# A weight tile's low half subtracted on GpSimd, and three bias groups of the second chunk moved into the first stage

## The chip, the cores and the metric

The kernel runs on one core of a Trainium2 chip. The metric is the device time of one execution in microseconds; a kernel's time is the median over its runs. Engines are named as in the profile: PE is TensorE's matmul side and PEld its weight loads, DVE is VectorE, ACT is ScalarE, POOL is GpSimd, SP issues all of this kernel's DMAs.

## What is computed

The reference is attention with a learned position bias, followed by two gated feed-forward layers:

```python
def _attn_ref(q, k, v, w1, b1, w2):            # q, k, v: (4, 8, 576, 64)
    scores = scale * np.matmul(q, k.transpose(0, 1, 3, 2))
    x = (psi_rel / psi_i)[..., None]           # from log1p of the positions alone
    h = np.maximum(x @ w1 + b1, 0.0)           # 32 hidden values for each pair of positions
    bias = h @ w2
    scores = scores + bias.transpose(2, 0, 1)[None, :, :, :]
    attn = np.exp(scores - np.max(scores, axis=-1, keepdims=True))
    attn = attn / (np.sum(attn, axis=-1, keepdims=True) + 1e-09)
    return np.matmul(attn, v)
def _moe_ref(x, w_gate, w_val, w_out):         # d_model 512, d_ff 1536
    return ((1.0 / (1.0 + np.exp(-(x @ w_gate)))) * (x @ w_val)) @ w_out
def _moe2_ref(x, w_in, w_out):                 # d_ff 2048
    h = x @ w_in
    return (h * np.clip(h + 3.0, 0.0, 6.0) / 6.0) @ w_out
```

The weights of the two layers are 64-bit floats in memory; the kernel converts them on the chip.

## The kernel before

The 576 query positions are cut into five chunks (128, 128, 128, 128, 64 positions; `QC`). For a chunk, attention has 16 units, each a pair of heads of one batch entry, and the feed-forward part has 68 steps (`STEPS`). A step multiplies one weight tile of 512 by 128 with the chunk's 512 tokens. Every operand is kept as two 32-bit halves, a high one (`xyh`, `gh`, `wp[:, 0]`) and a low one (`xyl`, `gl`, `wp[:, 1]`), so a step is 4 x 3 = 12 matmuls (`product`, L362).

The program has a **lead** and five blocks. In the lead, which an order written out by hand fixes on PE, ACT, DVE and SP, the bias of chunk 0 is computed in eight groups of 16 positions: `bias_hidden` (two relu tiles on ACT, L123, and two on DVE, L125), `bias_mm` (8 matmuls, L134, which the trace records as 16), `bias_out` (out of PSUM by ACT, L146, for chunk 1, and by DVE, L148, for the others, then a DMA to DRAM). `bias_read` fetches it back as tile `bm`. Then come chunk 0's 16 attention units: `att_qk` (L226), `att_min` (DVE, L241, from PSUM, with `bm`), `att_exp` (ACT, L251), `att_norm` (DVE, L258 to L261), `att_tr` (transposes L274, copies L277), `att_av` (L293) and `att_x` (L309, L310). 

Block k runs the 68 steps of chunk k. Between steps, a list of events (`block_events`) places the attention units of chunk k+1 and its bias; only PE's order is fixed by hand there, and the other engines' order is made by a scheduler. In block 0 each weight tile is also converted. `w_load` fetches the raw tile `wd` (pool `wf`), and `w_split` makes `wp` out of it: a scaled copy on ACT (L335), a shift and two bit operations on DVE (L336, L337, L340) in a work tile `cm`, of which there are two, then the high half on ACT (L345) and the low half on DVE (L346). `wp` (six buffers) is what the step's matmuls read; a DMA also writes it to DRAM (`wsp`, L347), from where the blocks 1 to 4 load it. Step i waits for tile i.

Conversions of tiles 0 and 1 stand in the lead, between the first `att_qk` and the first `att_min`. The tiles from 2 on belong to block 0, but the scheduler already puts some of them beside the lead's last units. PSUM holds two two-bank buffers (`s_ps`) for the bias groups and the scores, and four one-bank buffers for everything else.

Of the kernel before, what the change touches and what calls it, by code (L numbers as in the profile page):

```python
# [9 lines left out]
F32 = mybir.dt.float32  # L10
# [3 lines left out]
ALU = mybir.AluOpType  # L14
# [10 lines left out]
QC = ((0, 128), (128, 128), (256, 128), (384, 128), (512, 64))  # L25
# [30 lines left out]
def fused_kernel(ctx: ExitStack, tc: tile.TileContext, qd, kd, vd, tz, rd, zc, w2b, iden, wpack, out):  # L56
    nc = tc.nc
# [36 lines left out]
    t0 = S - QC[0][1]  # L94
# [65 lines left out]
    def bias_read(u):  # L160
        c, hp, b = u
        n = QC[c][1]
        if b == 0:
            bm = bm_p.tile([128, 2, S], F32, name="bm")
            for p in range(0, NQ, n):
                nc.sync.dma_start(out=bm[p:p + n], in_=biasD[c][:, 2 * hp:2 * hp + 2, :])
            bm_q[c, hp] = bm
# [159 lines left out]
    def w_split(n):  # L327

        if n >= NSTEP:
            return  # L330
        wd = wf_q.pop(n)
        low, high = wd[:, :, 0], wd[:, :, 1]
        m = A["cv"].tile([128, 512], U32, name="cm")
        f = m.bitcast(F32)
        nc.scalar.activation(out=f, in_=high.bitcast(F32), func=AF.Copy, scale=2.0 ** -112)  # L335
        nc.vector.tensor_scalar(out=m, in0=m, scalar1=3, scalar2=None, op0=ALU.logical_shift_left)  # L336
        nc.vector.scalar_tensor_tensor(  # L337
            out=m, in0=low, scalar=29, in1=m, op0=ALU.logical_shift_right, op1=ALU.bitwise_or
        )
        nc.vector.scalar_tensor_tensor(  # L340
            out=m, in0=high, scalar=0x80000000, in1=m, op0=ALU.bitwise_and, op1=ALU.bitwise_or
        )
        wp = w_p.tile([128, 2, 4, 128], F32R, name="wp")
        wv = wp.rearrange("p s c m -> p s (c m)")
        nc.scalar.activation(out=wv[:, 0], in_=f, func=AF.Copy)  # L345
        nc.vector.tensor_tensor(out=wv[:, 1], in0=f, in1=wv[:, 0].bitcast(F32), op=ALU.subtract)  # L346
        nc.sync.dma_start(out=wsp[n], in_=wv.bitcast(F32))  # L347
        wq[n] = wp

# [77 lines left out]
    ET = mybir.EngineType  # L427
    us = units[0]
    NL = len(us)
    with ExitStack() as lead:  # L430
        for name, bufs in (("s", 3), ("k", 6), ("v", 7), ("wf", 2), ("cv", 2)):
            A[name] = lead.enter_context(tc.tile_pool(name=name + "l", bufs=bufs))
        lead.enter_context(tc.manual_schedule(engines={ET.PE, ET.Activation, ET.DVE, ET.SP}))
        nc.sync.dma_start(out=id_t, in_=iden)
        for n in range(2):
            w_load(n)
        for u in us[0:3]:
            att_load(u, False)
        nc.sync.dma_start(out=tz_t[:, 0:t0], in_=tz[:, 0:t0])
        for G in range(QC[0][1] // 16 + 1):  # L440
            if G < QC[0][1] // 16:
                for g in range(4):
                    bias_hidden(G, g)
                bias_mm(G)
            if G:
                bias_out(G - 1)
        bias_read(us[0])
        att_qk(us[0])
        for n in range(2):
            w_split(n)  # L450
        att_min(us[0])
        att_qk(us[1])
        for n in range(NL + 2):
            if n + 3 < NL:
                att_load(us[n + 3])
            if n < NL:
                att_exp(us[n])
            if n + 1 < NL:
                att_min(us[n + 1])
            if 1 <= n <= NL:  # L460
                for part in range(3):
                    att_tr(us[n - 1], part, mm_ps)
            if n < NL:
                att_norm(us[n])
            if n >= 2:
                att_av(us[n - 2], mm_ps)
                att_x(us[n - 2])
            if n + 2 < NL:
                att_qk(us[n + 2])
            if n == NL - 4:  # L470
                gate = issued[0]

# [9 lines left out]
    for n in range(2, WA):  # L482
        w_load(n)

    def chunk_bias(c, t0, dt):

        i0, n = QC[c]
        G0, nG = i0 // 16, n // 16
        ev = []
        for g in range(nG):  # L490
            ev.append((t0 + dt * g, lambda G=G0 + g: [bias_hidden(G, t) for t in range(4)]))
        for g in range(0, nG, 2):
            def outs(G=G0 + g):
                for i in range(2):
                    bias_mm(G + i)
                for i in range(2):
                    bias_out(G + i)
            ev.append((t0 + dt * g + dt + 1, outs))
        return ev
# [24 lines left out]
    def block_events(k):  # L524
        ev = []
        last = NSTEP - 1
        if k < 2:
            ev += chunk_bias(k + 1, 2.0, 1.5)
            t0 = 21.0
            ev += chunk_att(k + 1, t0, last, 2)  # L530
        elif k + 1 < NC:
            ev += chunk_att(k + 1, 0.5, last, len(units[k + 1]) // 8)
        if 0 < k < NC - 2:
            ev += chunk_bias(k + 2, *((22.0, 5.2) if k == 1 else (4.0, 12.0)))
        return [e[::2] for e in sorted((e[0], n, e[1]) for n, e in enumerate(ev))]
# [79 lines left out]
```

## Time and profile before

| | us |
|---|---|
| median of 3 runs | 1197.76 (1196.39 to 1198.26) |
| the profiled execution's own time | 1193.32 |
| its span | 1191.2 |
| PE busy in the span | 1155.7 |
| DVE busy | 637.2 |
| ACT busy | 569.0 |
| POOL busy | 0.2 |

The profiled execution is 2.1 us longer than its span, and 4.4 us faster than the median. Busy time is a sum over stages that have different limits; a matmul's end is modelled, so that a busy PE is not necessarily PE at its peak.

### The profile page before, as it was taken

To read this page: it belongs to the slowest core of one execution; us is meant where nothing else is said; L and a number is where in the kernel's file an instruction comes from. 1 tells how busy PE (TensorE), PEld (TensorE's weight loads), DVE (VectorE), ACT (ScalarE), POOL (GpSimd) and SP (SyncE) were. 2 spreads that over 40 slices of the span, in tenths; PEclk is the share of its full clock that TensorE was granted. 3 is DMA by queue.
4 is the path that set the end of the run, shared out by engine and by line. 5 is a ranking of instruction groups with operands and counts; after the bars stand their busy time and mean duration, and the time that the engine had idled before them with its cause. 6 is when DMAs were issued, how large, how long until landed. Compare 5 with 4: busy or idle time off the path is not lost.

```text
span 1191.2 us, 20173 instructions
## 1 busy us (share of the span) xinstructions
PE 1155.7 (97%) x7676; PEld 926.0 (78%) x7676; DVE 637.2 (53%) x1384; ACT 569.0 (48%) x1153; POOL 0.2 (0%) x4
## 2 busy tenths in 40 slices
PE   5898998999999999999999999999999999999998
PEld 2666776777777787787788878878878878888998
DVE  6787888999973544574634453453323314231232
ACT  6686866677662434565633453443323314331231
POOL 0000000000000000000000000000000000000000
PEclk9899999999999999999999999999999999999999
DMA  6787899998977667676686666566677677658997
GB/s 228 275 308 257 306 328 323 365 342 313 338 263 236 205 227 224 194 226 199 188 272 196 213 194 218 187 215 192 188 230 234 208 239 220 212 167 257 368 365 275
DMA packets 115263, 297.64 MB, mean 250 GB/s; under 512 B 20448, under 2 KB 35168, under 8 KB 115168
## 3 DMA queue, kind: packets, MB, share of 16 engines
q1 hardware_dynamic: 115168, 296.36, 75.4%
q8 instruction: 61, 1.00, 0.3%
q14 instruction: 34, 0.28, 0.1%
HBM read 245.32 MB, written 50.99 MB: 249 GB/s over the span
## 4 chain that ended last, share of the span: by engine, by line
PE 83%; DVE 8%; DMA 5%; ACT 2%; issue 2%; SPq 0%; DVEq 0%; ACTq 0%
PE ps L362 63%; PE ps L293 6%; PE ps L274 5%; DMA wd<-wpack 3%; PE ps L226 3%; PE ps L210 3%; PE ps L134 2%; DVE cm L337 2%; DVE cm L340 1%; DVE wp L346 1%; DVE s L241 1%; ACT cm L335 1%; DMA wsp<-wp 1%; DVE cm L336 1%; DVE s L261 0%
## 5 line engine op out<-in xcount | busy, mean ns | idle before, releaser
L362 PE MATMUL ps<-xyh,wp 128*128 128x512 f32 (+1 forms) x1600 | 480.6, 375 | 0.0
L362 PE MATMUL ps<-gh,wp 128*128 128x512 f32 (+1 forms) x1120 | 345.7, 379 | 0.0
L362 PEld LDWEIGHTS ps<-xyh,wp 128*128 128x128 f32 x1600 | 290.5, 189 | 59.5 <-issue 8.2
L362 PE MATMUL ps<-xyl,wp 128*128 128x512 f32 (+1 forms) x800 | 295.0, 369 | 0.7 <-DVE xyl L375 0.7
L362 PEld LDWEIGHTS ps<-gh,wp 128*128 128x128 f32 x1120 | 204.1, 189 | 40.6 <-issue 6.4
L362 PE MATMUL ps<-gl,wp 128*128 128x512 f32 (+1 forms) x560 | 207.1, 370 | 0.0
L362 PEld LDWEIGHTS ps<-xyl,wp 128*128 128x128 f32 x800 | 151.2, 189 | 23.3 <-DVE xyl L375 1.1
L277 ACT ACTIVATE pT<-ps 128x384 f32<-128x384 f32 x216 | 101.4, 487 | 114.2 <-PE ps L274 113.7
L371 ACT ACTIVATE gh<-tmp 128x512 fp32r<-128x512 f32 (+1 forms) x140 | 82.3, 588 | 110.4 <-DVE tmp L393 76.7
L251 ACT ACTIVATE s<-s,m 128x576 f32<-128x576 f32 x144 | 110.5, 769 | 41.8 <-DVE m L241 41.7
L373 DVE TENSOR_TENSOR gl<-tmp,gh 128x512 fp32r<-128x512 f32 (+1 forms) x140 | 89.2, 637 | 62.7 <-ACT gh L371 62.4
L362 PEld LDWEIGHTS ps<-gl,wp 128*128 128x128 f32 x560 | 106.3, 190 | 14.9
L241 DVE CUSTOM_DVE_ANT_0 s<-ps,bm 128x576 f32<-128x576 f32 x144 | 103.8, 754 | 26.1 <-PE ps L226 13.5
L274 PE MATMUL ps<-id_t,s 128*128 128x128 f32 x648 | 102.6, 277 | 11.6 <-DVE s L261 10.2
L274 PEld LDWEIGHTS ps<-id_t,s 128*128 128x128 f32 x648 | 79.1, 141 | 43.2 <-issue 9.3
L293 PE MATMUL ps<-pT,vt 128*64 128x128 f32 (+1 forms) x1600 | 95.3, 267 | 1.0 <-ACT pT L277 1.0
L393 DVE SCALAR_TENSOR_TENSOR tmp<-tmp,ps 128x512 f32<-128x512 f32 (+1 forms) x60 | 38.0, 633 | 108.3 <-PE ps L362 107.3
L293 PEld LDWEIGHTS ps<-pT,vt 128*64 128x64 f32 x1600 | 78.7, 137 | 20.0 <-issue 14.4
L310 DVE TENSOR_TENSOR xyl<-ps,xyh 128x128 fp32r<-128x128 f32 x72 | 20.8, 289 | 117.0 <-ACT xyh L309 117.0
L399 DVE SCALAR_TENSOR_TENSOR tmp<-tmp,ps 128x512 f32<-128x512 f32 (+1 forms) x80 | 50.6, 632 | 60.8 <-ACT tmp L398 59.2
L261 DVE TENSOR_SCALAR s<-s,r 128x576 f32<-128x576 f32 x144 | 68.3, 516 | 1.9
L389 ACT ACTIVATE tmp<-ps 128x512 f32<-128x512 f32 (+1 forms) x60 | 33.2, 554 | 74.1 <-PE ps L362 72.1
(45 smaller groups left out, 857.0 us busy)
## 6 DMA issues: line engine op xcount, KB each, us to landing
wp<-wsp SPq DMA_DIRECT2D x272, 512.0 KB, 4.3
wd<-wpack SPq DMA_DIRECT2D x68, 512.0 KB, 5.6
wsp<-wp SPq DMA_DIRECT2D x68, 512.0 KB, 5.6
vt<-vd SPq DMA_DIRECT2D x80, 320.0 KB, 4.2
kt<-kd SPq DMA_DIRECT2D x80, 288.0 KB, 4.5
biasD<-bo SPq DMA_DIRECT2D x36, 288.0 KB, 2.7
bm<-biasD SPq DMA_DIRECT2D x16, 576.0 KB, 4.7
qt<-qd SPq DMA_DIRECT2D x16, 256.0 KB, 5.7
```

What stands on the lines that cost most here:

```text
L210: nc.tensor.matmul(out=ps[h][:, j, 0:NI], lhsT=x[r, b, :], rhs=y[r, NI * j:NI * j + NI], start=(i == 0), stop=(i == 2), tile_position=(64 ...
L241: nc.vector.tensor_tensor_reduce(out=d["s"][:, h].rearrange("p (a j) -> p a j", a=2), in0=ps[h][:, :, 0:NI], in1=bm[:, h].rearrange("p (a ...
L251: nc.scalar.activation(out=s[:, h], in_=s[:, h], func=AF.Exp, scale=-1.0, bias=d["m"][:, h:h + 1], accum_out=r[:, h:h + 1],)
L261: nc.vector.tensor_scalar(out=s[:, h], in0=s[:, h], scalar1=r[:, h:h + 1], scalar2=None, op0=ALU.mult)
L274: nc.tensor.transpose(out=ps[:, t * NQ:t * NQ + NQ], in_=p[:, 128 * k:128 * k + 128], identity=id_t)
L277: nc.scalar.activation(out=d["pt"][:, 3 * part:3 * part + 3], in_=ps[:, 0:3 * NQ].rearrange("p (t n) -> p t n", t=3), func=AF.Copy,)
L293: nc.tensor.matmul(out=po[64 * h:64 * h + 64, n * a:n * a + n], lhsT=vt[:, v], rhs=pt[:, k, n * a:n * a + n], start=(t == 0), stop=(t == 4 ...
L362: nc.tensor.matmul(out=ps[:, 0:nt], lhsT=w[:, c, :], rhs=x[:, 0:nt], start=(first and c == 0 and i == 0), stop=(last and c == 3 and i == 2),)
L371: nc.scalar.activation(out=hi[:, 0:nt], in_=src, func=AF.Copy, scale=scale)
L373: nc.vector.tensor_tensor(out=lo[:, 0:nt], in0=src, in1=hi[:, 0:nt].bitcast(F32), op=ALU.subtract)
L393: nc.vector.scalar_tensor_tensor(out=th, in0=th, scalar=1.0, in1=ps, op0=ALU.add, op1=ALU.mult)
L399: nc.vector.scalar_tensor_tensor(out=t, in0=t, scalar=6.0, in1=ps, op0=ALU.min, op1=ALU.mult)
```

## The change

The subtract that makes the low half (L346) goes from DVE to GpSimd, for all 68 tiles. In the lead, the first three of chunk 1's eight bias groups follow chunk 0's eight; block 0 then computes the other five, and its attention events start at step 16 where they started at step 21. The two conversions of the lead move from its beginning to its last two iterations. `NG0` is 8.

```diff
-        nc.vector.tensor_tensor(out=wv[:, 1], in0=f, in1=wv[:, 0].bitcast(F32), op=ALU.subtract)
+        nc.gpsimd.tensor_tensor(out=wv[:, 1], in0=f, in1=wv[:, 0].bitcast(F32), op=ALU.subtract)
...
+    NG0, NG1 = QC[0][1] // 16, 3
...
-        for G in range(QC[0][1] // 16 + 1):
-            if G < QC[0][1] // 16:
+        for G in range(NG0 + NG1 + 1):
+            if G < NG0 + NG1:
                 for g in range(4):
                     bias_hidden(G, g)
                 bias_mm(G)
             if G:
                 bias_out(G - 1)
-        bias_read(us[0])
+            if G == NG0:
+                bias_read(us[0])
         att_qk(us[0])
-        for n in range(2):
-            w_split(n)
         att_min(us[0])
...
                 att_qk(us[n + 2])
+            if n >= NL:
+                w_split(n - NL)
...
-    def chunk_bias(c, t0, dt):
+    def chunk_bias(c, t0, dt, done=0):
...
-        G0, nG = i0 // 16, n // 16
+        G0, nG = i0 // 16 + done, n // 16 - done
...
-            ev += chunk_bias(k + 1, 2.0, 1.5)
-            t0 = 21.0
+            ev += chunk_bias(k + 1, 2.0, 1.5, 0 if k else NG1)
+            t0 = 21.0 if k else 16.0
             ev += chunk_att(k + 1, t0, last, 2)
```

At the beginning of the lead, PE's order (L134 are the bias groups' matmuls, L226 the scores of the first units, L274 the transposes of unit 0), before with - and now with +:

```order
 L105 MATMUL ps<-zc_t,w2b_t 32x2 x2
-L134 MATMUL ps<-z,w2b_t 32x288 x64
+L134 MATMUL ps<-z,w2b_t 32x288 x88
 L226 MATMUL ps<-kt,qt 128x288 x12
 L274 MATMUL ps<-id_t,s 128x128 x9
```

The 24 matmuls of three groups now stand ahead of the first scores.

On ACT, the same place before (L123 are the bias groups' relu tiles, L335 and L345 conversions, L251 the first exponentials):

```order
L123 ACTIVATE z<-tz_t,zc_t,sc_t 128x576 x16
L335 ACTIVATE cm<-wd 128x512
L123 ACTIVATE z<-tz_t,zc_t,sc_t 128x576 x4
L345 ACTIVATE wp<-cm 128x512
L335 ACTIVATE cm<-wd 128x512
L345 ACTIVATE wp<-cm 128x512
L251 ACTIVATE s,r<-s,m 128x576 x4
```

And ACT's order there now (L146 copies a bias group of chunk 1 out of PSUM):

```order
L123 ACTIVATE z<-tz_t,zc_t,sc_t 128x576 x20
L146 ACTIVATE bo<-ps,cv_t 128x576
L123 ACTIVATE z<-tz_t,zc_t,sc_t 128x576 x2
L146 ACTIVATE bo<-ps,cv_t 128x576
L123 ACTIVATE z<-tz_t,zc_t,sc_t 128x576 x2
L146 ACTIVATE bo<-ps,cv_t 128x576
L123 ACTIVATE z<-tz_t,zc_t,sc_t 128x576 x2
L251 ACTIVATE s,r<-s,m 128x576 x4
```

Ten relu tiles and three copies stand behind the eight groups of chunk 0 now, where four relu tiles and two conversions stood; the last four relu tiles belong to groups 11 and 12, which the scheduler begins early.

At the end of the lead, ACT's order before, from the exponentials of unit 15 (L251) on (L277 and L309 belong to the last units, L389 is the tanh of step 0, L335 and L345 are conversions):

```order
L251 ACTIVATE s,r<-s,m 128x576 x2
L335 ACTIVATE cm<-wd 128x512
L277 ACTIVATE pT<-ps 128x384 x2
L345 ACTIVATE wp<-cm 128x512
L277 ACTIVATE pT<-ps 128x384
L335 ACTIVATE cm<-wd 128x512
L309 ACTIVATE xyh<-ps 128x128
L277 ACTIVATE pT<-ps 128x384 x3
L309 ACTIVATE xyh<-ps 128x128 x2
L389 ACTIVATE tmp<-ps 128x512
```

The same place in ACT's order now, from the same exponentials to the same tanh:

```order
L251 ACTIVATE s,r<-s,m 128x576 x2
L277 ACTIVATE pT<-ps 128x384 x3
L309 ACTIVATE xyh<-ps 128x128
L277 ACTIVATE pT<-ps 128x384 x3
L309 ACTIVATE xyh<-ps 128x128
L335 ACTIVATE cm<-wd 128x512
L345 ACTIVATE wp<-cm 128x512
L309 ACTIVATE xyh<-ps 128x128
L335 ACTIVATE cm<-wd 128x512
L345 ACTIVATE wp<-cm 128x512 x3
L335 ACTIVATE cm<-wd 128x512
L389 ACTIVATE tmp<-ps 128x512
```

The two conversions after unit 14's L309 are those of tiles 0 and 1; the high halves of tiles 2 and 3, whose first three operations still stand beside units 11 to 13, come behind them. No other tile is begun before step 0's tanh but one.

## Rows read from the trace of the kernel before

**Rows 1.** Stretches: us; busy us of PE, PEld, DVE, ACT, POOL; clock, DMA share, GB/s

```profile
78.00:99.60 21.60, 15.43 (x169) 12.22 (x167) 21.11 (x56) 18.26 (x45) 0.00 (x0) 1.00 0.96 357
99.60:137.50 37.90, 37.90 (x241) 27.92 (x239) 28.89 (x54) 26.29 (x43) 0.00 (x0) 1.00 0.74 256
137.50:190.00 52.50, 52.50 (x282) 40.90 (x280) 47.72 (x94) 36.30 (x63) 0.00 (x0) 1.00 0.91 322
190.00:365.80 175.80, 168.03 (x1035) 130.73 (x1032) 150.72 (x326) 114.19 (x238) 0.00 (x0) 0.99 0.92 324
```

**Rows 2.** Timeline, 0 to 50 us: start, us, engine, line, idle before and its releaser

```profile
22.39 3.13 ACT L123 ACTIVATE z<-tz_t,zc_t,sc_t 128x576 f32<-128x576 f32 x4
...
31.94 0.75 DVE L241 CUSTOM_DVE_ANT_0 s<-ps,bm 128x576 f32<-128x576 f32 x1
...
32.76 2.96 PE L226 MATMUL ps<-kt,qt 64*128 64x288 f32 x8 [6.64 <-DVE m L241]
...
38.79 2.13 PE L274 MATMUL ps<-id_t,s 128*128 128x128 f32 x9
```

**Rows 3.** PE alone by stretch, beginning of the lead: us, busy, granted clock, DMA

```profile
16.00:18.20 2.20, 0.44 (x4) 1.00 0.26 101
...
28.00:30.00 2.00, 0.00 (x0) 0.50 0.94 282
...
40.00:42.00 2.00, 2.00 (x13) 0.81 1.04 402
```

**Rows 4.** The chain that ended last, in order of time: start us, us, what

```profile
72.84 1.17 PE ps L226 x8
74.02 1.13 PE ps L274 x9
75.15 1.24 PE ps L293 x20
...
114.56 2.08 PE ps L134 x32
116.64 8.38 PE ps L362 x36
```

**Rows 5.** Timeline, 76 to 103 us, the end of the lead

```profile
94.91 0.94 DVE L261 TENSOR_SCALAR s<-s,r 128x576 f32<-128x576 f32 x2
...
101.34 0.50 PE L362 MATMUL ps<-xyh,wp 128*128 128x512 f32 x1
```

**Rows 6.** PE alone by stretch, round a stall of block 0

```profile
199.00:201.00 2.00, 0.00 (x0) 1.00 1.05 312
201.00:203.00 2.00, 1.81 (x6) 0.54 0.98 399
203.00:205.00 2.00, 2.00 (x7) 0.60 1.02 395
```

**Rows 7.** Groups, 99.6 to 365.8 us: busy us, mean ns of one, idle before

```profile
L346 DVE TENSOR_TENSOR wp<-cm,wp 128x512 fp32r<-128x512 f32 x62 | 42.2, 686 | 5.3 <-ACT wp L345 5.1
L337 DVE SCALAR_TENSOR_TENSOR cm<-wd,cm 128x512 uint32<-128x512 uint32 x60 | 41.1, 687 | 0.5
L340 DVE SCALAR_TENSOR_TENSOR cm<-wd,cm 128x512 uint32<-128x512 uint32 x60 | 41.1, 687 | 0.3
...
L336 DVE TENSOR_SCALAR cm<-cm 128x512 uint32<-128x512 uint32 x60 | 25.3, 423 | 13.1 <-ACT cm L335 12.9
...
L373 DVE TENSOR_TENSOR gl<-tmp,gh 128x512 fp32r<-128x512 f32 x28 | 19.2, 685 | 0.2
...
L261 DVE TENSOR_SCALAR s<-s,r 128x576 f32<-128x576 f32 x32 | 15.1, 515 | 0.2
```

**Rows 8.** Timeline, 176 to 215 us: one conversion in block 0

```profile
181.14 0.68 ACT L335 ACTIVATE cm<-wd 128x512 f32<-128x512 f32 x1
...
186.24 1.24 ACT L345 ACTIVATE wp<-cm 128x512 fp32r<-128x512 f32 x2 [1.26 <-DVE cm L340]
...
187.79 1.29 DVE L346 TENSOR_TENSOR wp<-cm,wp 128x512 fp32r<-128x512 f32 x2
```

More of the change, by code (lines that the diff above doesn't have):

```diff
@@ L492, in chunk_bias, with outs @@
         for g in range(0, nG, 2):
-            def outs(G=G0 + g):
-                for i in range(2):
+            def outs(G=G0 + g, two=min(2, nG - g)):
+                for i in range(two):
                     bias_mm(G + i)
-                for i in range(2):
+                for i in range(two):
                     bias_out(G + i)
```

## Prediction

> **What bounds the kernel now.** I read the engines' busy time by stretch first. Block 0, the only one with conversions, runs from 99.6 to 365.8 us. In its first 38 us PE never stops; from 190 us on it is idle for 175.8 - 168.03 = 7.8 us, while DVE is busy 86% of the time and the DMA engines 92% [rows 1]. So PE sets the pace here too, but from 190 us on it is now and then held up by work that comes through DVE. At the end of the lead the limit is another one: between 78 and 99.6 us PE is busy 15.43 of 21.60 us and DVE 21.11 [rows 1].
>
> The timeline of the beginning shows a third place. The first scores are done at about 26 us, then PE waits 6.64 us until DVE's first L241 at 31.94, which needs the bias back from DRAM [rows 2]. In that pause the granted clock falls to 0.50, the 1.2 GHz level, and it is back only between 40 and 42 us [rows 3]. The chain of waits gives PE's own prices at full clock: an attention unit 1.17 + 1.13 + 1.24 = 3.54 us, two bias groups (32 records) 2.08 us, three steps (36 matmuls) 8.38, so 2.79 a step [rows 4].
>
> **(a) The pause in the lead, -2.5 us.** Three groups of bias now stand ahead of the first scores on PE. They are paced by ACT. From 22.4 us on it has six relu tiles and three copies, and the first two tiles of group 11 stand ahead of the last copy. A relu tile takes 3.13/4 = 0.78 us [rows 2]; with the copies taken at the same price, 11 x 0.78 = 8.6 us, the last copy ends at 31.0. It frees the second PSUM buffer for unit 0's scores, and the last three of their four matmuls end at about 31.7. That is just ahead of 31.94, so I count the delay of the scores at nothing; the cover is the bias's way through DRAM, and if ACT needs 0.1 us more for each piece it is gone and costs up to 1 us. DVE and SP lose two conversions here, with their DMAs, and gain six relu tiles and three writes; both have less to do than before.
>
> PE's gaps become those of one group's pace on ACT, some 2 us, of which PE works 1.04. Between 16 and 18.2 us, where PE was nearly as empty, the clock stayed at 1.00 [rows 3]. So I expect the full clock through the start. There the eight pieces of a unit's scores took 2.96 us and unit 0's transposes 2.13 [rows 2], against 1.17 and 1.13 [rows 4]: 1.8 twice and 1.0 once, at most 4.6 us. DVE's minima and norms lie between these pieces and hide part. Bounds 0 (the clock falls all the same) and 4.6; I take 2.5.
>
> **(b) The end of the lead, +1.5 us.** Before, 68 - 62 = 6 low halves were done when step 0 began [rows 7]. Now tiles 2 and 3 get their first three operations beside units 11 to 13, and nothing more is converted until unit 14 is through. At 3.54 us a unit, unit 15's transposes, five units after those at 74.02, would stand at 91.7; with two tiles' 0.42 + 0.69 + 0.69 = 1.8 us on DVE in between I put them at about 93, where before the last norms ended at 95.85 [rows 5]. The attention ends at about 96.5. But step 0 waits for tile 0, whose L335 can start at about 95.4 behind unit 14's L309. It costs 0.68 + 0.42 + 0.69 + 0.69 + 0.62 [rows 7, 8] + 1.03 on POOL (see (d)), 4.1 us, and six handovers of some 0.13: ready at 100.3, against 101.34 before [rows 5]. Tile 1 is behind it on ACT and comes about 1 us after step 0's 2.79 us are over. So step 1 starts when it did. What is lost is clock: PE stands still for nearly 4 us, and after a stall that covered 199 to 201 us the clock was granted at 0.54 and 0.60 for two stretches of 2 us [rows 6], 1.7 us lost. Bounds 0 and 3; I take 1.5. All this stands 2.5 us earlier if (a) holds.
>
> **(c) Three groups less in block 0, -3.1 us.** 48 of the 128 bias records leave PE: 48/32 x 2.08 = 3.1 us [rows 4], at a place where PE never stopped. Six relu tiles on each of ACT and DVE, three copies and three DMAs go too. That attention starts at step 16 instead of 21 spreads it over more steps and moves none of it out of the block; I count it at nothing.
>
> **(d) The subtract on GpSimd, -3.5 us.** DVE loses 0.686 us for each of 66 tiles in block 0. No row shows a tensor operation on POOL. From below I bound its time by the same operation on DVE, 0.69 us [rows 7], from above by twice that, 1.37, and take 1.03. It lies on the tile's way to PE, and POOL has nothing else to do. What it does to DVE is open too. L337, L340, L336, L373 and L261 read two SBUF tensors or run faster than these, 0.42 us for the same shape; they are 141.8 us [rows 7] of the 227.3 - 42.2 = 185 us that stay on DVE [rows 1], 77%. If such operations can't run beside POOL's, each subtract blocks DVE for 0.77 x 0.69 = 0.53 to 0.77 x 1.37 = 1.05 us; if they can, for nothing. Between 0 and 1.05 I take 0.53. DVE then gains 0.16 x 66 = 10.6 us over the block, 7 of them after 190 us. PE is held up there by DVE, the DMAs and the conversion's own length, so I let half of it reach PE: -3.5.
>
> The Trainium skill (SBUF — State Buffer, Who interferes with whom) says that a VectorE instruction with two SBUF inputs, or in a two-port mode, and a GpSimd instruction that reads SBUF exclude each other for the whole instruction; no run here shows it so far. The Trainium skill (GPSIMD Engine Reference, Performance versus the Vector engine) gives 4497 ns for such an operation on 2048 elements; a quarter, 1.12 us, is an estimate. By both, a subtract blocks DVE for 0.77 x 1.12 = 0.86 us, more than the 0.686 it saves; (d) would be +3.8 and the sum about -0.3 us.
>
> **The sum.** -2.5 + 1.5 - 3.1 - 3.5 = -7.6 us. From the profiled execution's 1193.3 (a span of 1191.2 and 2.1 around it) that is 1185.7; that execution was 4.4 us under the median of the runs, so I set the same difference against the median: 1197.8 - 7.6 = 1190.
>
> **Rivals.** *DVE and POOL exclude each other, and POOL is slow* (the other side): at 1.37 us a subtract costs DVE 1.05 - 0.686 = 0.36 us net, 24 us over the block, 16 after 190 us, half on PE's path: (d) is +8, the sum +3.9, 1202. For it: 77% of DVE's work is of the kind that could be blocked. Against it: DVE has 14% idle time there to take it. It decides from a loss of 0.69 us for each subtract on; the range of losses crosses that.
>
> *No interference:* DVE loses all of 45 us, and what PE lost after 190 us, 7.8 us and the 1.7 of clock, is nearly all there is to win. The DMA share of 0.92 would rise towards 0.98, so I price it at -8: the sum is -12.1, 1186.
>
> *The first steps starve:* the six tiles in hand are gone, and the conversion's loop shows. With two `cm` tiles a new conversion waits for the subtract two before. In block 0 a tile took from 181.14 to 188.4, 7.3 us [rows 8], so 3.6 us each with two in flight, and the steps 0 to 15 want one every 2.79 + 0.33 us. 16 x 0.5 = 8 us lost: the sum is +0.4, 1198. For it: every step needs its tile, and POOL makes the loop longer. Against it: the 7.3 us were mostly queueing on a DVE full of attention, which isn't there yet; the bare pieces make 4.1 us, 2.1 each.
>
> **How the numbers follow.** I give the forecast 0.36, no interference 0.25, exclusion with a slow POOL 0.21, starving 0.18. About 0.2% (2.4 us) is what a measurement of this kernel can tell from no change. Faster takes in nearly all of the forecast, the case without interference and a fifth of the starving one: 0.62. Slower takes three quarters of the exclusion and a quarter of the starving: 0.21. The rest is 0.17. The range goes from 1182, the case without interference with all of (a), to 1204, exclusion with (a) at 1; the forecast's own is 1186 to 1194.
>
> **What would show it.** (a): the granted clock between 26 and 42 us, and whether the units' pace of 3.54 us begins earlier than before. (b): idle time of PE ahead of its first L362, released by POOL, and a dip of the clock after it. (c): 80 bias records in block 0. (d): the mean of L346 on POOL, those of L337, L340 and L373 against 0.69, DVE's busy time in the block, and whether PE's idle time after 190 us shrinks. I am wrong if DVE's operations grow by more than the subtract took, if L335 waits mostly for POOL, or if PE's wait at the end of the lead is much longer than 4 us.

## The result and the profile after

The changed kernel takes 1211.81 us (median of 4 runs, 1211.18 to 1213.04), beside 1197.08 for the kernel before, run beside it: a ratio of 1.0139, 95% interval 1.0123 to 1.0155. It is slower by 1.4%, where the forecast was 0.6% faster. The profiled execution took 1213.04 us, its span 1211.3. Line numbers are the same in both kernels; only L346 has moved to POOL.

The busy time by stretch, cut at the same places as [rows 1] (block 0 runs from 100.0 to 386.0 us here):

```profile
78.00:100.00 22.00, 17.42 (x190) 13.61 (x188) 15.43 (x44) 15.95 (x43) 0.00 (x0) 1.00 0.61 221
100.00:137.50 37.50, 36.88 (x204) 27.68 (x208) 32.02 (x47) 25.86 (x43) 14.70 (x12) 0.95 0.79 282
137.50:190.00 52.50, 46.49 (x229) 34.46 (x222) 47.07 (x74) 30.07 (x57) 19.02 (x14) 0.97 0.86 305
190.00:386.00 196.00, 182.57 (x1064) 139.91 (x1063) 168.43 (x298) 119.31 (x246) 59.78 (x43) 0.97 0.89 309
```

Block 0 has grown from 266.2 to 286.0 us; the blocks behind it are as long as they were. PE never stopped between 99.6 and 190 us before; now it is idle there for 0.62 + 6.01 us and for 13.43 us after. Its clock, once near 1.00, has a mean of 0.95 to 0.97 in all three stretches.

The groups of the same lines as in [rows 7], in block 0 alone (100 to 386 us):

```profile
L346 POOL TENSOR_TENSOR wp<-cm,wp 128x512 fp32r<-128x512 f32 x68 | 93.5, 1378 | 279.5 <-ACT wp L345 237.9 <-issue 15.1 <-PE ps L362 10.9
...
L340 DVE SCALAR_TENSOR_TENSOR cm<-wd,cm 128x512 uint32<-128x512 uint32 x65 | 56.3, 866 | 0.9
L337 DVE SCALAR_TENSOR_TENSOR cm<-wd,cm 128x512 uint32<-128x512 uint32 x65 | 56.0, 862 | 1.3
...
L335 ACT ACTIVATE cm<-wd 128x512 f32<-128x512 f32 x65 | 43.5, 669 | 21.3 <-POOL wp L346 16.3 <-DMA wd<-wpack 4.8
...
L345 ACT ACTIVATE wp<-cm 128x512 fp32r<-128x512 f32 x67 | 41.9, 628 | 45.0 <-DVE cm L340 40.4 <-PE ps L362 2.3 <-PE ps L274 2.1
L336 DVE TENSOR_SCALAR cm<-cm 128x512 uint32<-128x512 uint32 x65 | 37.0, 569 | 17.8 <-ACT cm L335 17.8
...
L261 DVE TENSOR_SCALAR s<-s,r 128x576 f32<-128x576 f32 x32 | 26.2, 861 | 0.3
...
L373 DVE TENSOR_TENSOR gl<-tmp,gh 128x512 fp32r<-128x512 f32 x28 | 24.2, 866 | 1.7 <-ACT gh L371 1.7
```

The operation on POOL has a mean of 1378 ns, twice the 686 of [rows 7]. DVE has lost it and gained nothing: its own operations have become longer, L340 from 687 to 866 ns, L337 to 862, L336 from 423 to 569, L261 from 515 to 861, L373 from 685 to 866. How this comes about is seen in the timeline of a few conversions (lines of DVE and POOL only):

```profile
108.81 0.68 DVE L340 SCALAR_TENSOR_TENSOR cm<-wd,cm 128x512 uint32<-128x512 uint32 x1
...
109.41 0.68 DVE L337 SCALAR_TENSOR_TENSOR cm<-wd,cm 128x512 uint32<-128x512 uint32 x1
...
110.24 1.31 POOL L346 TENSOR_TENSOR wp<-cm,wp 128x512 fp32r<-128x512 f32 x1 [2.69 <-ACT wp L345]
...
110.61 1.48 DVE L340 SCALAR_TENSOR_TENSOR cm<-wd,cm 128x512 uint32<-128x512 uint32 x1
...
116.67 1.41 POOL L346 TENSOR_TENSOR wp<-cm,wp 128x512 fp32r<-128x512 f32 x1 [2.54 <-ACT wp L345]
116.85 0.68 DVE L393 SCALAR_TENSOR_TENSOR tmp<-tmp,ps 128x512 f32<-128x512 f32 x1
...
119.45 1.29 POOL L346 TENSOR_TENSOR wp<-cm,wp 128x512 fp32r<-128x512 f32 x1 [1.37 <-ACT wp L345]
119.60 1.69 DVE L337 SCALAR_TENSOR_TENSOR cm<-wd,cm 128x512 uint32<-128x512 uint32 x1
```

L340 and L337 take 0.68 us while POOL is idle. The L340 that begins at 110.61, inside POOL's 110.24 to 111.55, ends at 112.09, 0.54 us after POOL does; the L337 at 119.60 ends at 121.29, 0.55 us after POOL's 120.74. They stand until POOL is through. L393, which takes one input from PSUM, runs its 0.68 us inside a subtract of POOL as if it weren't there. Over the whole trace, the 27 of L337 and L340 that begin inside a subtract of POOL have a mean of 1.54 us, and the 91 that touch none 0.69.

POOL waits as well, when DVE comes first:

```profile
335.91 0.68 DVE L337 SCALAR_TENSOR_TENSOR cm<-wd,cm 128x512 uint32<-128x512 uint32 x1
335.93 1.82 POOL L346 TENSOR_TENSOR wp<-cm,wp 128x512 fp32r<-128x512 f32 x1 [1.85 <-ACT wp L345]
...
336.72 1.58 DVE L340 SCALAR_TENSOR_TENSOR cm<-wd,cm 128x512 uint32<-128x512 uint32 x1
```

L337 began just ahead of POOL and keeps its 0.68 us, POOL's subtract takes 1.82 instead of its least, 1.27, and the L340 behind it is held again. So POOL's mean of 1378 ns has waiting in it.

Two more places that the prediction spoke of. The beginning, PE's timeline, DVE's first L241, and three stretches of the clock (answering [rows 2, 3]):

```profile
33.28 2.96 PE L226 MATMUL ps<-kt,qt 64*128 64x288 f32 x8 [1.03 <-DVE m L241]
...
39.32 2.18 PE L274 MATMUL ps<-id_t,s 128*128 128x128 f32 x9
```

```profile
32.46 0.76 DVE L241 CUSTOM_DVE_ANT_0 s<-ps,bm 128x576 f32<-128x576 f32 x1 [1.86 <-DMA bm<-biasD]
```

```profile
30.00:32.00 2.00, 1.08 (x7) 0.68 (x6) 0.60 (x2) 2.00 (x4) 0.00 (x0) 1.00 0.95 342
...
33.00:35.00 2.00, 1.72 (x6) 1.48 (x7) 0.90 (x4) 1.63 (x4) 0.00 (x0) 0.50 1.04 323
...
101.00:104.00 3.00, 2.67 (x6) 2.16 (x7) 1.95 (x3) 0.95 (x2) 0.52 (x2) 0.54 0.43 175
165.00:169.00 4.00, 3.32 (x9) 2.46 (x9) 3.96 (x7) 1.95 (x5) 1.93 (x2) 0.64 0.98 375
```

And the end of the lead, in the timeline from 95 to 104.5 us:

```profile
99.97 0.50 PE L362 MATMUL ps<-xyh,wp 128*128 128x512 f32 x1 [2.43 <-ACT wp L345]
...
100.00 1.27 POOL L346 TENSOR_TENSOR wp<-cm,wp 128x512 fp32r<-128x512 f32 x1 [99.56 <-ACT wp L345]
...
101.33 1.22 PE L362 MATMUL ps<-xyh,wp 128*128 128x512 f32 x2 [0.62 <-POOL wp L346]
```

The clock held through the pause in the lead, up to 33 us, and fell then, to the 1.2 GHz level, so unit 0's transposes begin at 39.32, later than the 38.79 of [rows 2]. Step 0 begins at 99.97 after 2.43 us without work, and the clock is near half (0.54) from 101 to 104. From 165 to 169 us, behind waits of 2.05 and 0.68 us for another tile, it is 0.64.

### The profile page after: what moved, and what is told of

Same layout as the page of the kernel before. It is cut to its first block, busy times and chain, and to the rows that moved or that the text cites. A ratio compares the mean times of both kernels' runs of the same rounds, so it can differ in the third digit from the quotient of the medians.

```text
span 1211.3 us, 20254 instructions
## 1 busy us (share of the span) xinstructions
PE 1170.2 (97%) x7676; PEld 932.0 (77%) x7676; DVE 649.9 (54%) x1316; ACT 568.8 (47%) x1153; POOL 93.7 (8%) x72
## 4 chain that ended last, share of the span: by engine, by line
PE 71%; DVE 2%; issue 0%; DMA 0%; ACT 0%; POOL 0%
PE ps L362 58%; PE ps L293 4%; PE ps L274 4%; PE ps L210 3%; PE ps L134 2%; PE ps L226 1%; DVE cm L337 0%; DVE cm L340 0%; DMA wp<-wsp 0%; DVE s L241 0%; DVE tmp L399 0%; DVE s L261 0%; DVE cm L336 0%; DVE gl L373 0%; POOL wp L346 0%
## 5 line engine op out<-in xcount | busy, mean ns | idle before, releaser
L362 PE MATMUL ps<-xyh,wp 128*128 128x512 f32 (+1 forms) x1600 | 485.9, 378 | 13.8 <-ACT wp L345 5.6
L277 ACT ACTIVATE pT<-ps 128x384 f32<-128x384 f32 x216 | 101.4, 487 | 115.3 <-PE ps L274 114.9
L251 ACT ACTIVATE s<-s,m 128x576 f32<-128x576 f32 x144 | 110.6, 770 | 40.7 <-DVE m L241 40.0
L373 DVE TENSOR_TENSOR gl<-tmp,gh 128x512 fp32r<-128x512 f32 (+1 forms) x140 | 94.3, 673 | 64.1 <-ACT gh L371 64.1
L241 DVE CUSTOM_DVE_ANT_0 s<-ps,bm 128x576 f32<-128x576 f32 x144 | 103.8, 752 | 28.9 <-PE ps L226 14.4
L346 POOL TENSOR_TENSOR wp<-cm,wp 128x512 fp32r<-128x512 f32 x68 | 93.5, 1378 | 279.5 <-ACT wp L345 237.9
L274 PE MATMUL ps<-id_t,s 128*128 128x128 f32 x648 | 103.4, 278 | 0.9 <-ACT s L251 0.4
L274 PEld LDWEIGHTS ps<-id_t,s 128*128 128x128 f32 x648 | 79.2, 141 | 30.9 <-issue 6.2
L293 PEld LDWEIGHTS ps<-pT,vt 128*64 128x64 f32 x1600 | 80.2, 138 | 24.8 <-issue 16.3
L393 DVE SCALAR_TENSOR_TENSOR tmp<-tmp,ps 128x512 f32<-128x512 f32 (+1 forms) x60 | 37.9, 632 | 106.6 <-PE ps L362 105.9
L261 DVE TENSOR_SCALAR s<-s,r 128x576 f32<-128x576 f32 x144 | 79.4, 593 | 2.1
```

The lines of the kernel that those rows point to most:

```text
L241: nc.vector.tensor_tensor_reduce(out=d["s"][:, h].rearrange("p (a j) -> p a j", a=2), in0=ps[h][:, :, 0:NI], in1=bm[:, h].rearrange("p (a ...
L251: nc.scalar.activation(out=s[:, h], in_=s[:, h], func=AF.Exp, scale=-1.0, bias=d["m"][:, h:h + 1], accum_out=r[:, h:h + 1],)
L261: nc.vector.tensor_scalar(out=s[:, h], in0=s[:, h], scalar1=r[:, h:h + 1], scalar2=None, op0=ALU.mult)
L274: nc.tensor.transpose(out=ps[:, t * NQ:t * NQ + NQ], in_=p[:, 128 * k:128 * k + 128], identity=id_t)
L277: nc.scalar.activation(out=d["pt"][:, 3 * part:3 * part + 3], in_=ps[:, 0:3 * NQ].rearrange("p (t n) -> p t n", t=3), func=AF.Copy,)
L293: nc.tensor.matmul(out=po[64 * h:64 * h + 64, n * a:n * a + n], lhsT=vt[:, v], rhs=pt[:, k, n * a:n * a + n], start=(t == 0), stop=(t == 4 ...
```

## The experiments

The theory after the result: POOL's subtract and DVE's operations on two SBUF tensors exclude each other; DVE, which heads the way of every tile to PE in block 0, is later for it, and PE waits. Rivals: the tile's way is longer by POOL's slower operation (latency alone); the `cm` loop of two buffers turns slower; the moved conversions, the moved bias groups or the earlier attention cost the time.

**1. The change without GpSimd.** Only L346 back:

```diff
-        nc.gpsimd.tensor_tensor(out=wv[:, 1], in0=f, in1=wv[:, 0].bitcast(F32), op=ALU.subtract)
+        nc.vector.tensor_tensor(out=wv[:, 1], in0=f, in1=wv[:, 0].bitcast(F32), op=ALU.subtract)
```

> The change with the subtract back on VectorE; bias groups, conversions and attention events stay where the change put them. Interference theory (while GpSimd subtracts, VectorE's operations with two SBUF inputs or in the faster mode stand still): the loss goes with the subtract, so 1190 to 1195 us, a little under before. Loop theory (two work tiles, and a tile's way to PE is longer over GpSimd): the same. Placement theory (attention from step 16 on and no tiles in hand at step 0 cost the time): still 1203 us or more.

1189.94 us (1189.04 to 1191.1), a ratio of 0.9949 [0.9934, 0.9964] to the kernel before: the rest of the change gains 6.3 us, and GpSimd costs 21.9. Its stretches of block 0, which ends at 362.6:

```profile
98.20:137.50 39.30, 39.30 (x220) 29.24 (x221) 36.37 (x66) 29.18 (x49) 0.00 (x0) 0.96 0.84 300
137.50:190.00 52.50, 48.21 (x242) 36.49 (x242) 45.42 (x93) 32.72 (x61) 0.00 (x0) 0.97 0.92 325
190.00:362.60 172.60, 170.94 (x1034) 132.52 (x1029) 152.54 (x328) 114.32 (x235) 0.00 (x0) 1.00 0.94 337
```

Against these the change's block is 21.6 us longer. PE is idle for 20.06 us in it, here for 0 + 4.29 + 1.66 = 5.95: 14.1 more. It is busy for 36.88 + 46.49 + 182.57 = 265.9 us against 258.45: 7.5 more for the same matmuls. By the means of the clock the change loses 0.05 x 37.5 + 0.03 x 52.5 + 0.03 x 196 = 9.3 us to the lower level, this kernel 0.04 x 39.3 + 0.03 x 52.5 = 3.1: about 6 of those 7.5, as the means have two digits. So some two thirds of GpSimd's price are waits, and most of the rest is the lower clock.

What PE waits for in block 0 (us in all, times, the longest), in the change and then in this run:

```profile
PE ps L362 <- ACT wp L345: 5.6, 3, 2.4
PE ps L293 <- ACT pT L277: 3.0, 3, 1.5
PE ps L362 <- POOL wp L346: 2.6, 3, 1.3
PE ps L362 <- ACT pT L277: 2.5, 1, 2.5
```

```profile
PE ps L362 <- ACT wp L345: 3.6, 2, 2.4
PE ps L362 <- DVE wp L346: 3.1, 3, 1.8
```

The first line of each holds the 2.43 us ahead of step 0. So the waits for a weight tile are 8.2 us in the change and 6.7 here. The other waits are 14.3 us there and 1.5 here, and they make nearly all of the difference: PE waits for attention's copies (L277) and for the feed-forward part's own operations on ACT and DVE. The theory has the delay on the way of the weight tiles; these rows say that it comes in mostly through everything else that passes DVE and ACT. ACT waits 40.4 us for L340 ahead of L345 in the change and 18.7 here, and what stands behind L345 on ACT is later for it. That this is the path is read from the rows; no run tests it alone.

**2. The subtract on GpSimd alone,** in the kernel before:

```diff
-        nc.vector.tensor_tensor(out=wv[:, 1], in0=f, in1=wv[:, 0].bitcast(F32), op=ALU.subtract)
+        nc.gpsimd.tensor_tensor(out=wv[:, 1], in0=f, in1=wv[:, 0].bitcast(F32), op=ALU.subtract)
```

> The kernel before with nothing changed but the subtract on GpSimd. Interference and loop theory: slower than before by 12 to 22 us, 1209 to 1219 us, with the means of L337 and L340 at 0.82 us or more. Placement theory: 1201 us or less.

1204.95 us, a ratio of 1.0077 [1.0057, 1.0097], 8.7 us over the 1196.22 of the kernel before, run beside it, and less than the 12 to 22 expected. The groups show the same growth, and PE's longest waits are for attention's norms (6.6 us in all in the kernel before), none for a weight tile:

```profile
L346 POOL TENSOR_TENSOR wp<-cm,wp 128x512 fp32r<-128x512 f32 x68 | 97.6, 1436 | 266.6 <-ACT wp L345 223.9 <-PE ps L362 12.9 <-issue 10.0
...
L340 DVE SCALAR_TENSOR_TENSOR cm<-wd,cm 128x512 uint32<-128x512 uint32 x68 | 62.9, 925 | 1.2
```

```profile
PE ps L274 <- DVE s L261: 11.6, 5, 5.2
```

So the subtract loses wherever it stands, but 8.7 us here and 21.9 in the change. Part of that difference is found in runs 8 to 12.

**3. More of the suspected cost.** The kernel of run 1 with an extra subtract on GpSimd into a scratch tile that nothing reads (`sh`, a new pool of one buffer); its own L346 stays on DVE:

```diff
+        sh = A["sh"].tile([128, 512], F32, name="sh")
+        nc.gpsimd.tensor_tensor(out=sh, in0=tz_t[:, 0:512], in1=wv[:, 0].bitcast(F32), op=ALU.subtract)
```

> The change with the subtract back on VectorE, and after it a second subtract of the same size on GpSimd that reads the high half and a constant tile and writes a scratch tile that nothing reads. No tile's way to PE gets longer by it. Interference theory: 12 to 30 us slower than the same kernel without the second subtract, and VectorE's L337, L340 and L336 grow as in the change. Loop theory: within 3 us of the kernel without it.

1233.67 us, a ratio of 1.0311 [1.0293, 1.0328]: 43.7 us more than run 1, beyond the 12 to 30 expected, though no tile's way has an operation more. DVE's operations are longer (busy 692.5 us in all, against 637.0):

```profile
L348 POOL TENSOR_TENSOR sh<-tz_t,wp 128x512 f32<-128x512 f32 x68 | 117.3, 1726 | 276.7 <-ACT wp L345 273.5 <-ACT xyh L373 2.3
...
L346 DVE TENSOR_TENSOR wp<-cm,wp 128x512 fp32r<-128x512 f32 x68 | 64.1, 948 | 4.0 <-ACT wp L345 3.4
```

The longest of POOL's subtracts takes 3.95 us, while four such operations of DVE, one behind the other, pass at 0.68 us each. One thing besides has changed: POOL's read holds `wp` longer, and L345 waits for it six times, 13.1 us in all. In run 4 that wait is 8.4 us.

**4. Work on POOL that doesn't read.** The same place; POOL copies one column, so that it starts when the subtract would, and then only writes:

```diff
+        sh = A["sh"].tile([128, 512], F32, name="sh")
+        nc.gpsimd.tensor_copy(out=sh[:, 0:1], in_=wv[:, 0, 0:1].bitcast(F32))
+        for _ in range(3):
+            nc.gpsimd.memset(sh, 0.0)
```

> The change with the subtract on VectorE and, in place of the second subtract of the earlier run, GpSimd work that hardly reads: a copy of one column of the high half, then three fills of a scratch tile of 512 columns. Interference by reads (only an operation of GpSimd that reads two tensors stands in VectorE's way): within 3 us of 1189.9 us, L337 and L340 at 0.69 us. If any work on GpSimd stands in its way: 10 us slower or more, and L336, L337 and L340 grow.

1193.84 us (1189.64 to 1195.5, 10 runs), 0.9979 [0.9969, 0.999]; 3.9 us over run 1, where at most 3 was expected. The profiled execution is the fastest of the ten, with a span of 1187.9, that of run 1. POOL is busier than in run 3 (157.3 us in all against 117.5):

```profile
L350 POOL MEMSET sh<- 128x512 f32 x204 | 116.4, 571 | 11.7 <-POOL sh L348 0.2
...
L337 DVE SCALAR_TENSOR_TENSOR cm<-wd,cm 128x512 uint32<-128x512 uint32 x68 | 46.6, 686 | 0.6
L340 DVE SCALAR_TENSOR_TENSOR cm<-wd,cm 128x512 uint32<-128x512 uint32 x68 | 46.5, 685 | 0.3
L346 DVE TENSOR_TENSOR wp<-cm,wp 128x512 fp32r<-128x512 f32 x68 | 46.1, 684 | 4.0 <-ACT wp L345 3.4
...
L336 DVE TENSOR_SCALAR cm<-cm 128x512 uint32<-128x512 uint32 x68 | 33.8, 498 | 8.1 <-ACT cm L335 7.6
```

The three operations on two SBUF tensors stay at 684 to 686 ns; only L336, the fast one with one input (421 ns in run 1), and L261 (516 to 530) grow, and DVE is busy for 643.4 us instead of 637.0. So it is POOL's reading that holds up the others. The Trainium skill (SBUF — State Buffer, Who interferes with whom) says so: a VectorE instruction with two SBUF inputs contends with a GpSimd instruction that reads SBUF, not with one that only writes, and that one in a two-port mode contends with GpSimd. Runs 3 and 4 agree, with 948 against 684 ns for L346.

**5. The tile's way alone.** The kernel of run 1; POOL copies one column and then subtracts one column of the low half, so that the tile is complete about when it was in the change, but POOL holds hardly anything:

```diff
-        nc.vector.tensor_tensor(out=wv[:, 1], in0=f, in1=wv[:, 0].bitcast(F32), op=ALU.subtract)
+        nc.vector.tensor_tensor(out=wv[:, 1, 1:512], in0=f[:, 1:512], in1=wv[:, 0, 1:512].bitcast(F32), op=ALU.subtract)
+        sh = A["sh"].tile([128, 1], F32, name="sh")
+        nc.gpsimd.tensor_copy(out=sh, in_=wv[:, 0, 0:1].bitcast(F32))
+        nc.gpsimd.tensor_tensor(out=wv[:, 1, 0:1], in0=f[:, 0:1], in1=wv[:, 0, 0:1].bitcast(F32), op=ALU.subtract)
```

> The change with the subtract on VectorE for 511 of 512 columns; GpSimd copies one column into a spare tile and then subtracts the last column, some 1.2 us after the high half is there. So a tile reaches TensorE about as late as with the whole subtract on GpSimd, but GpSimd holds its inputs only for one column. If the longer way of a tile is what cost the time, this run comes to 1200 us or more. If VectorE being held up is what cost it, it stays at 1190 to 1194, with L337 and L340 near 0.69 us.

1191.83 us (1190.18 to 1194.1, 10 runs), 0.9968 [0.9957, 0.9978], 1.9 us over run 1. The two operations on POOL make 597 + 445 = 1.04 us in the mean, and DVE is as it was:

```profile
L340 DVE SCALAR_TENSOR_TENSOR cm<-wd,cm 128x512 uint32<-128x512 uint32 x68 | 46.5, 684 | 0.4
...
L348 POOL COPY sh<-wp 128x1 f32<-128x1 f32 x68 | 40.6, 597 | 285.6 <-ACT wp L345 285.5
...
L349 POOL TENSOR_TENSOR wp<-cm,wp 128x1 fp32r<-128x1 f32 x68 | 30.3, 445 | 0.0
```

Their means have POOL's waiting for DVE in them: the least times are 179 ns for the copy and 184 for the subtract, and the longest copy, 2.91 us, stands while six operations of DVE on SBUF follow one another at their usual length. Tile by tile, the low half is complete 1.59 us behind the end of L345 in the mean, against 1.56 in the change and 1.41 in run 1. So this run has the change's longer way, and that way is worth some 2 us of the 21.9; latency alone falls as the cause.

**6. Half of the columns.** The kernel of run 1 with columns 256 to 511 of the subtract on GpSimd:

```diff
-        nc.vector.tensor_tensor(out=wv[:, 1], in0=f, in1=wv[:, 0].bitcast(F32), op=ALU.subtract)
+        for eng, s in ((nc.vector, slice(0, 256)), (nc.gpsimd, slice(256, 512))):
+            eng.tensor_tensor(out=wv[:, 1, s], in0=f[:, s], in1=wv[:, 0, s].bitcast(F32), op=ALU.subtract)
```

> The change with half of the subtract's columns on VectorE and half on GpSimd. With VectorE held up in proportion to GpSimd's time, L337 and L340 grow by half of what they grew in the change (to about 0.77 us), VectorE saves half an operation, and half of GpSimd's 21.9 us is lost: 1200 us, or less if the shorter way of a tile takes the clock drops away. If the lock is taken once for each operation whatever its length, the loss stays near 20: 1208.

1197.87 us, 1.002 [1.0008, 1.0032]: 7.9 us over run 1, 36% of the 21.9, where the number of POOL's operations is the same and their time 71%. So there is no fixed price for each operation (1208 expected), but the loss isn't in proportion to POOL's time either. Half the columns take POOL 983 ns, and DVE's own half takes 585:

```profile
L347 POOL TENSOR_TENSOR wp<-cm,wp 128x256 fp32r<-128x256 f32 x68 | 66.8, 983 | 289.9 <-ACT wp L345 271.9 <-PE ps L363 4.7 <-PE ps L293 4.3
...
L347 DVE TENSOR_TENSOR wp<-cm,wp 128x256 fp32r<-128x256 f32 x68 | 39.7, 585 | 5.8 <-ACT wp L345 5.3
```

L337 (734) and L340 (706) grew less than the 0.77 us expected. POOL's half and DVE's half become ready at the same moment, so part of the meeting is now between the two: DVE's half takes from 0.40 to 0.99 us.

**7. A third `cm` buffer,** in the change, block 0 only:

```diff
-    for name, bufs in (("wf", 3), ("cv", 2)):
+    for name, bufs in (("wf", 3), ("cv", 3)):
```

> The change with three work tiles for the conversion in block 0 in place of two. Loop theory: most of the loss comes back, 1197 to 1203 us, and ScalarE's L335 hardly waits for GpSimd any more. Interference theory: within 4 us of the change, 1208 to 1214 us.

1209.12 us, 1.0108 [1.0093, 1.0123], 2.7 us less than the change. L335's wait for POOL goes from 16.3 to 9.5 us, but L340 keeps its length (873 ns over the whole kernel, 858 in the change). The loop of the two tiles is a small part.

**8 to 12. What GpSimd costs in other orders.** Five kernels tell the change's other parts apart. Run 8 is run 1 with attention from step 21, run 9 the change with attention from step 21:

```diff
-            t0 = 21.0 if k else 16.0
+            t0 = 21.0
```

> The change with the subtract on VectorE and the attention events of block 0 starting at step 21 again, as before. If the earlier start is worth something by itself, this is slower than the same kernel with step 16 (1189.9 us), by 1 to 3 us; if it is worth nothing, 1188 to 1191 us.

> The change itself (subtract on GpSimd) with attention starting at step 21. In the kernel before, GpSimd's subtract alone cost 8.7 us, in the change 21.9. If the earlier attention makes it dear (VectorE full from step 16 on, with no tiles in hand), this one is faster than the change by 5 to 12 us, 1200 to 1207 us. If the interference alone decides, with the order of the work of no account, within 3 us of the change, 1209 to 1214 us.

Run 10 is run 8 without the three groups in the lead, so that of the change only the two moved conversions are left:

```diff
-    NG0, NG1 = QC[0][1] // 16, 3
+    NG0, NG1 = QC[0][1] // 16, 0
```

> The change with the subtract on VectorE, attention from step 21 and no bias groups moved: the kernel before with its first two conversions at the end of the lead. If the three groups are worth their 3.1 us of matmul time in block 0, this is 3 us slower than the kernel with three groups and step 21; if moving the two conversions is worth nothing, 1195 to 1198 us.

Runs 11 (the change) and 12 (run 1) have the two conversions back ahead of the first units:

```diff
         att_qk(us[0])
+        for n in range(2):
+            w_split(n)
         att_min(us[0])
...
-            if n >= NL:
-                w_split(n - NL)
```

> The changed kernel with its two first conversions back where they stood, ahead of the first units of the lead; subtract on GpSimd, three bias groups in the lead and attention from step 16 stay. Moving the two conversions cost 7.6 us with the subtract on VectorE (two steps of the order without them compared). If GpSimd's dear price in the change (21.9 us, against 8.7 in the kernel before) comes from tiles that the first steps no longer have in hand, this run gains more than that move: 1197 to 1201 us, 9 to 13 us over its VectorE counterpart. If the price is contention on VectorE alone, it stays near 20 us over the counterpart: 1203 to 1206. Either way the mean of L346 on POOL stays near 1.4 us and L337 and L340 near 0.85.

> The same order with the subtract on VectorE: of the change only the three bias groups in the lead and attention from step 16 are left. From the runs so far the groups are worth 6.8 us and attention from 16 is worth 7.0, so by their sum 1197 - 13.8 = 1183 us; 1187 if the two overlap (both relieve the same stretch), and 1190 if the move of the conversions was in truth harmless in this order.

Run 8 is 7.0 us slower than run 1, where 1 to 3 was expected, and run 10 another 6.8, where 3 was expected. Run 9 lies in the range that was given for interference alone, so the earlier attention isn't the most of GpSimd's price. Run 12 came out above all three of its values. The medians in us, with each kernel's ratio to the runs of the kernel before that were made beside it, and the price of GpSimd in each order (the numbers in brackets are the runs above):

| first two conversions | groups in the lead | attention from | subtract on DVE | subtract on GpSimd | price |
|---|---|---|---|---|---|
| ahead of unit 0 | 0 | 21 | before, 1196.22 | (2) 1204.95, 1.0077 [1.0057, 1.0097] | 8.7 |
| ahead of unit 0 | 3 | 16 | (12) 1194.97, 0.9994 [0.9984, 1.0005] | (11) 1206.74, 1.0091 [1.0077, 1.0106] | 11.8 |
| end of the lead | 3 | 21 | (8) 1196.91, 1.0014 [1.0003, 1.0024] | (9) 1213.46, 1.0143 [1.0124, 1.0161] | 16.6 |
| end of the lead | 3 | 16 | (1) 1189.94, 0.9949 [0.9934, 0.9964] | the change, 1211.81, 1.0139 [1.0123, 1.0155] | 21.9 |
| end of the lead | 0 | 21 | (10) 1203.69, 1.0063 [1.0047, 1.008] | | |

GpSimd costs 9 to 12 us where six low halves are ready when step 0 begins, and 17 to 22 where the first two conversions stand at the lead's end and none is. Block 0 of the profiled executions grows by 12.2, 14.8, 16.1 and 21.6 us in the same order, so the direction is the same and the steps are smaller. Run 11 was to show that: its price of 11.8 lies in the 9 to 13 that tiles in hand would give, though its time lies above both of the ranges expected, since its counterpart (run 12) was dearer than the sum of the parts. So the place of the two conversions changes the price; that it does so by the tiles in hand is not shown, as GpSimd adds little to PE's waits for a weight tile in either place (8.2 against 6.7 us above, none in runs 11 and 12).

That sum is the miss of this series. With the subtract on DVE, the moved conversions cost 7.5 us in the order of before (1203.69 - 1196.22) and gain 5.0 in the order of the change (1189.94 against 1194.97). Run 12 shows a part of why. In its timeline of DVE:

```profile
36.47 0.69 DVE L346 TENSOR_TENSOR wp<-cm,wp 128x512 fp32r<-128x512 f32 x1 [0.69 <-ACT wp L345]
37.08 0.75 DVE L241 CUSTOM_DVE_ANT_0 s<-ps,bm 128x576 f32<-128x576 f32 x1
```

With three more groups ahead of them, the conversions hold DVE until 37.1 us, and unit 0's minima start at 37.08, and PE's second scores wait 6.47 us for them; in the change they start at 32.46. In the kernel before, the same work lay in the wait for the bias, and the minima started at 31.94 [rows 2]. In the profiled executions, moving the conversions brings step 0 forward by 5.7 us here (103.86 in run 12, 98.17 in run 1) and by 2.2 in the order of before (99.65, and 97.43 in run 10); it makes block 0 longer by 4.4 us here and by 10.8 there. So the lead explains 3.5 us of the swing. The larger part lies in block 0, and no run says why.

## Why the prediction was wrong, point by point

**(d) is the step that failed**: "Between 0 and 1.05 I take 0.53 [...] I let half of it reach PE: -3.5." It is +21.9 in the order of the change. Three things in it were off.

*The loss for each subtract.* In block 0 the five lines that I had named as open to blocking grew, against run 1, where they took 44.5 (L340), 44.5 (L337), 27.3 (L336), 15.1 (L261) and 19.1 us (L373), by 11.8 + 11.5 + 9.7 + 11.1 + 5.1 = 49.2 us, 0.72 for each of 68 subtracts. That lies between my bounds, but past the 0.69 at which I had the sign turn. POOL's own time, 1.27 us at the least and 1.38 in the mean with its waits for DVE, was at the upper bound and not in the middle. The Trainium skill (GPSIMD Engine Reference, Performance versus the Vector engine), from whose figure I had estimated 1.12, was nearer than the middle, and the sum by both pages, with (d) at +3.8, had the sign of this step right.

*What DVE saves.* I counted 0.686 us for a subtract gone. The rows of the change at 108.81 and 109.41 show that two such operations in a row start 0.60 us apart, though each is recorded with 0.68. So 68 of them free some 41 us, an estimate. (In block 0 they were 62 before and are 68 now, not 66.) DVE lost more than it saved: it was busy for 649.9 us, in run 1 for 637.0.

*How much of it reaches PE.* I took half. DVE's added busy time and the added time of the kernel, pair by pair: 8.7 and 8.7 us (run 2), 14.8 and 11.8 (11 against 12), 8.1 and 7.9 (6), 12.5 and 16.6 (9 against 8), 12.9 and 21.9 (the change), 55.5 and 43.7 (3), 6.4 and 3.9 (4). That is 0.6 to 1.7 us of kernel for each us of DVE, about one for one in the middle, and the tiles in hand don't order it (runs 3 and 6 have none and lie at 0.8 and 1.0). DVE had 14% idle time, but this gave it no room to catch up; L336 waits 17.8 us for L335, an operation of the same chain, so I read that idle time as its handovers. The lower clock is in these sums; in the change it is a little under a third of the 21.9.

The rival *DVE and POOL exclude each other* had the mechanism and the sign. Its price was too high for each subtract (1.05 us lost, measured 0.72) and far too low for the kernel (+8).

**(a), -2.5, didn't come in the profiled execution of the change.** The clock stayed at 1.00 through the pause, as forecast, and the first minima came 0.5 us late; but PE's small gaps after them, 1.03 us and less, then went with a fall to half at 33 us. In the profiled execution of run 4 it did not fall there, and the same scores took 1.91 us instead of 2.96:

```profile
32.97 1.91 PE L226 MATMUL ps<-kt,qt 64*128 64x288 f32 x8 [1.05 <-DVE m L241]
```

Its step 0 began at 95.94, that of run 1 at 98.17: 2.2 us, close to the size of (a), in one pair of executions. Why it holds in one execution and not in another is open. The gaps on PE ahead of the fall are alike.

**(b), +1.5.** By itself, in the order of before, the move cost 7.5 us (run 10). I set my 100.3 for step 0 against 101.34, which is where its matmuls go on behind the last unit's; step 0 had begun at 99.65, so by my own figures, before (a), it came later and not earlier. PE's wait was 2.43 + 0.62 us and not "nearly 4", since the first matmuls need only the high half; the dip of the clock came as forecast, from 101 to 104. What I missed is what the tiles in hand were worth later: with the subtract on DVE block 0 is 4.4 us longer in run 1 (264.4) than in run 12 (260.0), and 10.8 longer in run 10 than in the kernel before.

**(c), -3.1, and attention from 16, counted at nothing.** The 80 bias records of L134 are left in block 0. The groups are worth 6.8 us (run 8 against 10), the start at 16 another 7.0 (run 1 against 8), both with the conversions at the lead's end; with them ahead of unit 0 the two together are worth 1.3 us (run 12 against the kernel before). "Moves none out of the block" was true of the work and missed what it does: fewer units for each later step, and so, as I read it without a test, less queueing on DVE ahead of the conversions. With the subtract on GpSimd the same start at 16 gains 1.6 us only (the change against run 9).

Taken together, (a), (b) and (c) were forecast at -4.1 us, and the change without GpSimd measured -6.3. The sign of the forecast fell with (d), but that the rest came near is luck: it is 7.5 for the moved conversions, -6.8 for the groups with the start of the lead, and -7.0 for attention from 16, where I had 1.5, -5.6 and 0. The range had a slip as well: 1186 less the rest of (a), 2.1 us, is 1184 and not 1182.

*The first steps starve* was no empty rival: PE, which never stopped in this stretch before, is idle for 6.01 us between 137.5 and 190 us, and L335 waits mostly for POOL (16.3 of 21.3 us in the block). But run 1 is idle there for 4.29 us without GpSimd, its L335 waits 12.5 us for the subtract on DVE, and a third `cm` tile gives back only 2.7 us. *No interference* fell with run 3 and with the growth of DVE's own operations.

**What stays open.** It is open by which path DVE's lost time reaches PE, and why GpSimd costs more with the conversions at the lead's end. Why attention from step 16 adds to GpSimd's price where it relieves DVE otherwise was only argued (more operations that can be held up, where no tiles are in hand). The version that beats both kernels is run 1.

## What to carry to other kernels

Work moved from VectorE to GpSimd has left it only if GpSimd doesn't read SBUF beside VectorE operations on two SBUF tensors; otherwise set GpSimd's duration, times the share of such operations, as an upper bound of the loss (here 0.77 x 1.38 = 1.06 us, measured 0.72) against the pitch of the operation removed (the time from its start to that of the next), not its recorded length. Idle time of an engine that feeds the bound one need not absorb a loss: here 1 us more on VectorE cost the kernel 0.6 to 1.7 us, with the fallen clock in it. And price a moved piece of work in the order in which it will stand: the same two conversions cost 7.5 us in one order and gained 5.0 in another.

## What the runs showed of the hardware

- Operations of 128x512 with two SBUF inputs follow each other on VectorE every 0.60 us while each is recorded with 0.68; where the second needs the first's result, in run 12, L337 and L340 start 0.73 us apart (31.18 and 31.91).
- A GpSimd subtract and a VectorE operation on two SBUF tensors exclude each other both ways: the L340 that came second took 1.48 us instead of 0.68, and GpSimd's subtract, where it came second, 1.82 instead of 1.27.
- GpSimd's subtract takes at the least 184 ns for one column (run 5), 730 for 256 (run 6) and 1270 for 512 (the change), nearly one line: some 0.18 us and 2.1 ns a column, an estimate. Beside a busy VectorE the means are 445, 983 and 1378. A memset of 128x512 takes 521 ns at the least and 571 in the mean, a copy of one column 179 and 597.
- GpSimd work that only writes left the operations on two SBUF tensors at 684 to 686 ns, but slowed the fast one with one input from 421 to 498.
